# A written-out order for the first six steps of a recurrence and its router: a dozen moves, waits for a shared port, and router weights loaded earlier

## The chip, the cores and the metric

The kernel runs on one core of a Trainium2 chip. The core has five engines that work side by side, each on its own instructions in order: TensorE (PE in the profile, with its weight loads shown as PEld), VectorE (DVE), ScalarE (ACT), GpSimd (POOL) and SyncE (SP). SP issues nearly all the loads. The metric is the time of one execution on the device, in microseconds (us).

## The reference

Two stages follow each other, all in 32-bit floats. The first is a gated linear recurrence over 768 steps for 4 batches of 8 heads with 48 channels:

```
f = 1 / (1 + exp(-f_logit))
state = f[t] * state + outer(k[t], v[t])
y[t] = q[t] @ state
```

The second is a mixture of experts without dropping, over the 3072 rows that y makes with its heads side by side (384 columns). Each row goes to the one of 8 experts with the largest logit:

```
logits = x @ w_gate;  e = argmax(logits);  g = softmax(logits)[e]
out = g * (relu(x @ w1[e]) @ w2[e])
```

with w1[e] of 384 by 1024 and w2[e] of 1024 by 384.

## The kernel before

The recurrence is done in chunks of 128 steps. Twelve units of work are numbered 0 to 11: each is one chunk of two batches, which holds 16 heads, two to a slot of 128 partitions, in 8 slots of 128 steps. The units of one pair of batches are every second one, so the state of unit u comes from unit u - 2.

For one unit u the steps are these; the names are those that the change uses, with the line of the kernel before:

- lf, lk, lq, lv (L466, on SP): load f, k, q and v. The tiles are reused: f has two, k three, q four, v three. So a load waits for the last reader of an earlier unit's tile.
- exp and ln (L476, L484, on ACT): the negative logarithm of the gate.
- scan (L491, on DVE): its running sum over the chunk.
- r and dec (L505, L520, on ACT): the growth and the decay, exp of plus and minus the sum.
- byr (L509): k times r, on POOL (for unit 0 on DVE). byd (L532, on DVE): q times the decay.
- ends and last (L515, L527, on POOL): small copies of the last sum and the last decay.
- sc, in halves a and b (L543, on PE): scores of the chunk, k against q. mask (L549, on DVE): copies the causal ones to `at`.
- kp (L558, on PE) and keep (L563, on ACT): the transposed k, brought out of PSUM.
- wi, in halves (L571, on PE): the part of y from within the chunk. bef (L592, on PE): the part from the state before it.
- dp (L608, on PE): what the chunk adds to the state. upd (L623 or L625, on DVE) adds it to the old state, and updp (written upd..p; L627, on POOL) multiplies by the last decay.
- set (L633, on ACT): brings y out of PSUM. xp (L663, on PE): turns the rows and makes the logits in one product with a matrix that holds the router weights. The logits are summed over the slots on DVE (lg, L671), and lay (L688, L693, on ACT) brings the rows out.
- oh (choose, L214 to L222, on DVE), wgh (weigh, L254, on ACT), place (place and fill, L233 to L260, on DVE) and send (L189, indirect DMAs of POOL): the expert of each row, its place, and the scatter of the rows to DRAM, for two units at a time.

kp, dp, xp and a few others take turns at two banks of PSUM (`turns`), so each waits until what was two turns before is read.

The whole stage stands in an order written by hand (`manual_schedule`): on each engine the instructions run in the order in which the Python code issues them, and semaphores that the framework sets make an instruction wait for what it reads or overwrites. A first part of the code does units 0 and 1 and begins 2 and 3. Then a loop over n from 1 to 13 does the step n: the scores of unit n, the "within" and "before" of unit n - 1, the rows and logits of unit n - 2, and the elementwise work of units n + 1 to n + 3, with special cases for n = 1, 2 and 3.

The constants (`load_consts`, L174, 473.5 KB) and the router weights (`load_gate`, L180, four pieces of 6 KB) are written to one tile, `fpack`. The loop's products of k and r can be given one more wait: `by_r` (L507) takes an instruction out of the list `routed` and waits for it ("the port of both").

After the units, the eight experts follow, each with 24 groups of matmuls by w1 (`widen`, L316) and by w2 (`narrow`, L332); leftover rows are gathered in groups of 32 (L1081, L1107).

Of the kernel before, what the change touches and what calls it, by code (L numbers as in the profile page):

```python
# [1 line left out]

# [8 lines left out]
F32 = mybir.dt.float32  # L11
# [3 lines left out]
OP = mybir.AluOpType  # L15
# [103 lines left out]
def _bc(ap, axis, n):  # L119
    shape = list(ap.shape)  # L120
    shape.insert(axis, n)
    return ap[tuple([slice(None)] * axis + [None])].to_broadcast(shape)
# [3 lines left out]
def kernel(  # L126
# [41 lines left out]
    def load_first_consts():  # L168
        nc.scalar.dma_start(mpack, nc.inline_tensor(mv, name="c_mpack").ap())
        nc.scalar.dma_start(ident, fdram[:, slice(*fat["ident"])])  # L170
# [236 lines left out]
    def load_pads(e):  # L407
# [10 lines left out]
        tc.declare_no_dep(ins, group="xs", reason="no row is written twice")  # L418
        tc.add_to_no_dep_group("xs", ins)

    with ExitStack() as st:
        ld = st.enter_context(tc.tile_pool(name="ld", bufs=1))
        wk = st.enter_context(tc.tile_pool(name="wk", bufs=2))
# [21 lines left out]
            nc.vector.memset(g[:, :, 0:1], 0.0)  # L445
        units = [{} for _ in range(NU)]
        routed = []
        SYNC = mybir.DependencyInfo(mybir.DependencyClass.Sync, mybir.DependencyReason.DATA)
        states = [None, None]
        used = [0, 1]  # L450
# [6 lines left out]
        def load(u, names, parts=(slice(None),)):  # L457
            x = units[u]
            for n in names:
                src = {"q": qu, "k": ku, "f": fu, "v": vu}[n]  # L460
                if n == "v":
                    x[n] = ld.tile([128, 2, H, D], F32, name=n, bufs=3)
                else:
                    x[n] = held[n][u % len(held[n])]
                for part in parts:
                    nc.sync.dma_start(x[n][:, part], src[u][:, part])  # L466
# [19 lines left out]
        def total(u, part=whole):  # L486

            x = units[u]
            if "sum" not in x:
                x["sum"] = wk.tile([128, SEG, CR], F32, name="sum")  # L490
            nc.vector.tensor_tensor_scan(  # L491
                x["sum"][:, part].rearrange("p s c -> p (s c)"),
                x["g"][:, part].rearrange("p s c -> p (s c)"),
                cap[:, part].rearrange("p s c -> p (s c)"),
                0.0,
                OP.add,
                OP.min,
            )

        def growth(u, part=whole):  # L500

            x = units[u]
            if "r" not in x:
                x["r"] = wk.tile([128, SEG, C], F32, name="r", bufs=1)
            nc.scalar.activation(x["r"][:, part], x["sum"][:, part, 1:CR], AF.Exp)  # L505
# [8 lines left out]
        def ends(u):  # L514
            nc.gpsimd.tensor_copy(rend[:, u], units[u]["sum"][:, :, C])  # L515
# [7 lines left out]

        def last_decay(u):
            x = units[u]
            x["last"] = wk.tile([128, SEG], F32, name="last", bufs=3)
            nc.gpsimd.tensor_copy(x["last"], x["dec"][:, :, C - 1])  # L527

        def by_decay(u, part=whole):
            x = units[u]  # L530
            q = x["q"][:, part]
            nc.vector.tensor_tensor(q, q, x["dec"][:, part], op=OP.mult)  # L532

        def heads():
            return [(p, h, slice(DP * h, DP * h + DP)) for p in range(HP) for h in range(2)]
# [29 lines left out]
        def within(u, a):  # L565

            x = units[u]
            if a == 0:
                x["yt"] = yt
            for p, h, _ in heads():  # L570
                nc.tensor.matmul(  # L571
                    x["yt"][DP * (h ^ a) : DP * (h ^ a) + D, a, p],
                    lhsT=x["v"][:, a, 2 * p + h],
                    rhs=x["at"][:, a, h, p],
                    start=p == 0,
                    stop=x["old"] is None,
                    skip_group_check=True,
                )
# [38 lines left out]
        def update(u):  # L617

            x = units[u]
            new = wk.tile([128, SEG, D], F32, name="state", bufs=4)  # L620
            last = _bc(x["last"], 2, D)
            if x["old"] is None:
                nc.vector.tensor_copy(new, x["dp"])  # L623
            else:
                nc.vector.tensor_tensor(new, x["dp"], x["old"], op=OP.add)  # L625
            states[u % 2] = new
            return lambda: nc.gpsimd.tensor_tensor(new, new, last, op=OP.mult)  # L627

        def settle(u):
            x = units[u]  # L630
# [64 lines left out]
        st.enter_context(tc.manual_schedule(engines=ordered))  # L695

        nc.scalar.preload_act_table_set("natural_log_exp_and_others")
        load(0, "f", ab)
        load(0, "kq")
        load(1, "f")  # L700
        load_first_consts()
        load(1, "kq")
        for i in (1, 0):
            nc.gpsimd.memset(scores[i], 0.0)
        def warm(count):

            for _ in range(count):
                nc.tensor.matmul(yt[:, 0, 0], lhsT=pad[:, 0:C], rhs=pad[:, 0:C], start=True, stop=True)

        warm(24)  # L710
        for part in ab:
            steps(0, part)
            total(0, part)
        load(2, "f")
        load(0, "v")
        for part in ab:
            growth(0, part)
            by_r(0, part, nc.vector)
            decay(0, part)
            by_decay(0, part)  # L720
        ends(0)
        last_decay(0)
        for part in ab:
            steps(1, part)
        load(3, "f")
        load(2, "k")
        load(1, "v")
        load(2, "q")
        load(3, "q")

        def early_banks():

# [38 lines left out]
            del sends[: len(now)]  # L771


        score(0, 0)
        score(0, 1)
        keys(0)
        warm(12)
        for part in ab:
            total(1, part)
        for a in range(2):  # L780
            for h in range(2):
                mask(0, a, h)
        for part in ab:
            growth(1, part)
            by_r(1, part)
        for part in ab:
            decay(1, part)
            by_decay(1, part)
        ends(1)
        last_decay(1)  # L790
        steps(2)
        total(2)
        keep(0)
        steps(3, logs=False)
        growth(2)
        load_consts()
        load(3, "k")
        load(4, "f")
        load(2, "v")
        load(5, "f")  # L800
        load_gate()

        for n in range(1, NU + 2):
            here, back, last = n, n - 1, n - 2
            ahead = n + 1 < NU
            state = n < NU - 2
            rt = None
            if here < NU:
                units[here]["old"] = states[here % 2]
            if 2 <= last:  # L810
                settle(last)
            if later and later[0] < NU - 1:
                later[1].weigh()
            if here < NU:
                for a in range(2):
                    score(here, a)
            if ahead and n != 2:
                by_r(n + 1)
                ends(n + 1)
            if decayed:  # L820
# [3 lines left out]
                scatter_some(n)  # L824
            if n == NU - 2:
                soon = [load_rows(first[e]) for e in range(EARLY)]
            if n == 1:
                units[0]["old"] = None
                added(0)
                update(0)()  # L830
            if ahead and not 1 < n < 4:
                decay(n + 1)
                last_decay(n + 1)
            if state:
                keys(here)
                keep(here)
            if n == 2:
                growth(n + 1)
                by_r(n + 1)
                ends(n + 1)  # L840
            if 1 < n < 4:
                decay(n + 1)
                last_decay(n + 1)
            if here < NU:
                for a in range(2):
                    for h in range(2):
                        mask(here, a, h)
            if n == 1:
                log(3)
                within(0, 0)  # L850
                within(0, 1)
                settle(0)
            if n + 3 < NU:
                steps(n + 3)
            if later and n >= NU - 1:
                settled(*later)
                later = None
                scatter_some(NU)
            if 2 < n < NU - 2:
                total(n + 2)  # L860
            if n == NU - 2:
                by_decay(n + 1)
            first_half = 1 < n < NU - 2
            if first_half:
                within(back, 0)
            if 0 <= last:
                rt = rows(last, later[1] if later else None)
                lay(last)
            if later and n == NU - 2:
                settled(*later)  # L870
                later = None
                scatter_some(NU)
            if ahead and n < NU - 2:
                by_decay(n + 1)
            if n == 2:
                total(n + 2)
            if rt:
                rt.choose()
                if n < NU - 2:
# [7 lines left out]
            for a in range(int(first_half), 2):  # L887
                if 0 < back < NU:
                    within(back, a)
            if n == 2:  # L890
                settle(1)
            if n + 2 < NU and n != 1:
                growth(n + 2)
            if n == NU + 1:
                widen(soon[0], weights[0], early_h, range(3, 7))
# [2 lines left out]
            if state:  # L898
                added(here)
                decayed = update(here)  # L900
            if n == 1:
                total(3)
            if back < NU:
                before(back)
            if rt:
# [9 lines left out]
            if n == NU + 1:  # L915
                widen(soon[0], weights[0], early_h, range(7, NF))
                turn(soon[1])
            if n == 1:
                load(n + 3, "q")
            if n + 3 < NU:  # L920
                load(n + 3, "k")
            if n + 2 < NU:
                load(n + 2, "v")
            if 1 < n and n + 3 < NU:
                load(n + 3, "q")
            if n + 5 < NU:
                load(n + 5, "f")
            if n == 1:
                load_first_pads()
            if n in (8, 9):  # L930
                load_first_weights(n - 8)
                load_second_weights(n - 8)
# [395 lines left out]
```

## Time and profile before

| What | Value |
|---|---|
| median of 10 runs | 389.91 us (389.46 to 389.99) |
| the profiled execution's own time | 389.94 us |
| its span, first to last instruction | 388.2 us |
| busy: PE, DVE, ACT, POOL | 376.2, 169.3, 103.0, 115.8 us |
| DMA traffic | 95.05 MB, mean 245 GB/s |
| granted TensorE clock, mean | 0.997 |

A row of the timeline reads: start in us, time in us, engine, line, operation, what it writes and reads (out<-in), how many instructions were merged, and in brackets how long the engine had been idle before it and what ended that. SPq, ACTq and POOLq are instructions of an engine's queue, such as the issue of a DMA; the transfer itself lasts on after it. The chain is the work that ended last, followed back from the last instruction; it is printed in order of time. In the slices each digit is a fortieth of the span, 9.7 us, in tenths.

### The profile page before, as it was taken

The page shows a single profiled execution, that of the slowest core. Times are in us where ns is not written, and L with a number is a line of the kernel's source. Part 1 is how long each engine was busy: PE and PEld are TensorE (multiplying, and loading weights), DVE is VectorE, ACT ScalarE, POOL GpSimd, SP SyncE. Part 2 cuts the span into 40 slices and gives each one's busy share as a digit, 9 for nine tenths or more (in the row PEclk, how much of TensorE's full clock was granted, in tenths as well). Part 3 has the DMA queues.
Part 4 walks back from the last instruction along what each step waited for, and adds up shares of the span by engine and source line. Part 5 has one row for each costly group of instructions (what it writes and reads, how often), then busy time and mean ns, then how long its engine had stood idle before and what let it go on. Part 6 is the DMA issues. An engine that isn't in the chain of part 4 may idle for free.

```text
span 388.2 us, 7727 instructions
## 1 busy us (share of the span) xinstructions
PE 376.2 (97%) x3062; PEld 264.8 (68%) x3062; DVE 169.3 (44%) x365; ACT 103.0 (27%) x190; POOL 115.8 (30%) x118
## 2 busy tenths in 40 slices
PE   7988999999999999999999999999999999999993
PEld 7877899999989778685555555654466456555452
DVE  6998988889764632112121131115412113111360
ACT  6888878775432001010100110000010000001000
POOL 5378868887706710101102101100210210210113
PEclk9999999999999999999999999999999999999998
DMA  7999667868973659795559799899164359993141
GB/s 290 399 351 354 196 229 256 280 207 300 389 252 112 219 139 305 200 319 108 195 158 383 213 394 394 212 403 249 41 222 135 102 192 392 397 416 141 22 163 64
DMA packets 51516, 95.05 MB, mean 245 GB/s; under 512 B 20824, under 2 KB 40731, under 8 KB 49424
## 3 DMA queue, kind: packets, MB, share of 16 engines
q1 hardware_dynamic: 48016, 84.76, 64.5%
q0 software_dynamic: 3168, 9.64, 6.7%
q8 instruction: 25, 0.41, 0.4%
q14 instruction: 19, 0.16, 0.1%
q10 hardware_dynamic: 288, 0.08, 0.1%
HBM read 79.46 MB, written 15.21 MB: 244 GB/s over the span
## 4 chain that ended last, share of the span: by engine, by line
PE 88%; DMA 5%; DVE 2%; SPq 1%; issue 1%; ACT 1%; POOL 0%; POOLq 0%; DVEq 0%; ACTq 0%
PE hps L316 28%; PE yps L332 24%; PE yps L1107 7%; PE xp L663 6%; PE yt L571 5%; PE s L543 4%; PE s L316 3%; PE hps L1081 3%; PE yp L332 3%; PE yt L592 3%; DMA fpack<-c_fpack 2%; DMA f<-in_fu_dram 2%; PE dp L608 2%; PE kp L558 2%; DMA fpack<-in_moe_w_gate_dram 1%; SPq L466 1%
## 5 line engine op out<-in xcount | busy, mean ns | idle before, releaser
L316 PE MATMUL hps<-xT,w1t 128*128 128x352 f32 (+2 forms) x384 | 110.1, 447 | 0.0
L316 PEld LDWEIGHTS hps<-xT,w1t 128*128 128x128 f32 x384 | 72.7, 190 | 37.3 <-issue 2.2
L332 PE MATMUL yps<-w2t,hT 128*128 128x384 f32 x288 | 94.4, 487 | 0.0
L189 POOL DMA_INDIRECT out_dram<-ysb,dst x24 | 23.3, 972 | 222.3 <-DVE ysb L343 212.5
L332 PEld LDWEIGHTS yps<-w2t,hT 128*128 128x128 f32 x288 | 54.6, 190 | 38.6 <-issue 1.5
L326 ACT ACTIVATE hT<-hps 128x352 f32<-128x352 f32 (+2 forms) x28 | 13.7, 491 | 200.7 <-PE hps L316 190.6
L328 DVE TENSOR_SCALAR hT<-hps 128x352 f32<-128x352 f32 (+2 forms) x28 | 15.6, 558 | 92.9 <-PE hps L316 92.9
L343 DVE TENSOR_SCALAR ysb<-yps,tg 128x384 f32<-128x384 f32 x22 | 13.6, 618 | 74.4 <-PE yps L332 55.7
L189 POOL DMA_INDIRECT xs<-xr,posi x24 | 32.3, 1345 | 19.3 <-DVE counts L233 13.3
L549 DVE COPY_PREDICATED at<-mpack,s 128x512 f32<-128x512 uint8 x48 | 31.1, 728 | 6.1 <-PE s L543 6.1
L509 POOL TENSOR_TENSOR k<-k,r 128x1024 f32<-128x1024 f32 (+1 forms) x12 | 26.5, 2215 | 19.7 <-ACT r L505 10.3
L491 DVE TENSOR_TENSOR_SCAN sum<-g,cap 128x1032 f32<-128x1032 f32 (+1 forms) x14 | 28.8, 2058 | 2.9 <-ACT g L484 2.8
L1107 PE MATMUL yps<-qw,hqT 128*32 128x192 f32 (+1 forms) x192 | 26.8, 380 | 0.0
L663 PE MATMUL xp<-fpack,ys 128*128 128x104 f32 x192 | 25.1, 281 | 1.0 <-DMA fpack<-in_moe_w_gate_dram 0.8
L543 PE MATMUL s<-q,k 64*128 64x128 f32 x384 | 24.7, 278 | 1.4 <-POOL last L527 0.8
L571 PE MATMUL yt<-at,v 128*48 128x128 f32 x384 | 25.1, 276 | 0.0
L543 PEld LDWEIGHTS s<-q,k 64*128 64x128 f32 x384 | 22.4, 188 | 3.3 <-issue 1.5
L663 PEld LDWEIGHTS xp<-fpack,ys 128*128 128x128 f32 x192 | 22.7, 191 | 2.8 <-issue 1.3
L571 PEld LDWEIGHTS yt<-at,v 128*48 128x48 f32 x384 | 20.0, 123 | 2.6 <-issue 1.5
L1107 PE MATMUL yps<-w2t,hT 128*32 128x384 f32 x192 | 21.4, 487 | 0.0
L1107 PEld LDWEIGHTS yps<-w2t,hT 128*32 128x32 f32 x192 | 7.6, 110 | 13.0 <-issue 12.5
L532 DVE TENSOR_TENSOR q<-q,g 128x1024 f32<-128x1024 f32 (+1 forms) x14 | 16.4, 1174 | 0.0
(114 smaller groups left out, 361.6 us busy)
## 6 DMA issues: line engine op xcount, KB each, us to landing
qw<-in_moe_w_dram SPq DMA_DIRECT2D x16, 1536.0 KB, 12.3
w1t<-in_moe_w_dram SPq DMA_DIRECT2D x8, 1536.0 KB, 7.1
w2t<-in_moe_w_dram SPq DMA_DIRECT2D x8, 1536.0 KB, 12.6
k<-in_ku_dram SPq DMA_DIRECT2D x12, 512.0 KB, 4.7
q<-in_qu_dram SPq DMA_DIRECT2D x12, 512.0 KB, 5.7
f<-in_fu_dram SPq DMA_DIRECT2D x11, 512.0 KB, 6.0
xs<-pad SPq DMA_DIRECT2D x8, 600.0 KB, 4.4
v<-in_vu_dram SPq DMA_DIRECT2D x12, 384.0 KB, 4.9
```

The source lines that it names most:

```text
L189: ins = nc.gpsimd.indirect_dma_start(out=dst, out_offset=bass.IndirectOffsetOnAxis(ap=idx, axis=0), in_=src, in_offset=None, bounds_check= ...
L316: nc.tensor.matmul(x["h"][:, f], lhsT=w[0][:, j, b * 128 : b * 128 + 128], rhs=x["xT"][:, j], start=j == 0, stop=j == KD - 1,)
L328: nc.vector.tensor_scalar(to, x["h"], 0.0, None, op0=OP.max)
L332: nc.tensor.matmul(yp, lhsT=x["hT"][:, f, t * C : t * C + C], rhs=w[1][:, f, :], start=f == 0, stop=f == NF - 1,)
L491: nc.vector.tensor_tensor_scan(x["sum"][:, part].rearrange("p s c -> p (s c)"), x["g"][:, part].rearrange("p s c -> p (s c)"), cap[:, part ...
L509: ins = on.tensor_tensor(k, k, units[u]["r"][:, part], op=OP.mult).ins
L532: nc.vector.tensor_tensor(q, q, x["dec"][:, part], op=OP.mult)
L543: nc.tensor.matmul(ps[h][:, p], lhsT=x["k"][r, s], rhs=x["q"][r, s], start=True, stop=True)
L549: nc.vector.copy_predicated(x["at"][:, a, h], _bc(causal, 1, HP), x["ps", a][h])
L571: nc.tensor.matmul(x["yt"][DP * (h ^ a) : DP * (h ^ a) + D, a, p], lhsT=x["v"][:, a, 2 * p + h], rhs=x["at"][:, a, h, p], start=p == 0, st ...
L663: nc.tensor.matmul(xp[:, p], lhsT=x["ys"][:, a, p], rhs=wx[:, p, 0:XW] if a else wx[:, p, E:WX], start=True, stop=True,)
L1107: nc.tensor.matmul(yp[r], lhsT=h[:, f, at : at + T], rhs=w[:, f, cols], start=f == 0, stop=f == NF - 1, skip_group_check=True,)
```

## The change

The first part and the loop's steps n = 1 to 5 are replaced by a string of steps, `FIRST_STEPS`, that a small table of functions (`DO`) carries out one by one; the loop begins at n = 6. The same steps are there with the same shapes, but for six warm-up matmuls fewer (`fill6` for `warm(12)`), and a fourth buffer for `last`. By engine these are moved:

- PE: kp 2 stands between the two halves of score 2. In steps 3 and 5 both halves of "within" come before xp, and bef comes before dp.
- DVE: scan 5 comes before the masks of unit 3 instead of after them.
- ACT: ln 4 comes behind lay 0 (it was right behind exp 4), with ln 5 behind it.
- POOL: ends 0 comes behind k1's products; ends 3 before k3's; the state multiplications of units 2, 3 and 4 one or two places later; a send behind a small copy.
- SP: the four router weights' loads come right behind the constants, ahead of lk 3, lf 4, lv 2 and lf 5.

Besides, each k product of units 1 to 6 waits for the latest scan, q product, choice or placing issued before it on DVE (`port["latest"]`). In the loop before, only those behind a choice or a placing did (units 5 and on).

```diff
+    FIRST_STEPS = """
+        lf0a lk0 consts0 lq0 lf1 lk1 lq1 fill24 exp0a ln0a scan0a exp0b lf2 lv0 ln0b scan0b
+        r0a byr0a dec0a byd0a r0b byr0b dec0b byd0b last0 exp1a ln1a exp1b lf3 lk2 lv1 lq2
+        lq3 consts1 gate0 ln1b sc0a sc0b kp0 fill6 scan1a scan1b mask0a mask0b r1a byr1a r1b
+        byr1b ends0 dec1a byd1a dec1b byd1b ends1 last1 exp2 ln2 scan2 keep0 exp3 r2 sc1a
+        sc1b byr2 ends2 dp0 lk3 lf4 lv2 lf5 upd0 upd0p dec2 last2 kp1 lq4 lk4 keep1 mask1a
+        mask1b ln3 wi0a wi0b lv3 set0 exp4 lf6 pads0 byd2 dp1 upd1 scan3 sc2a upd1p kp2 sc2b
+        keep2 r3 ends3 byr3 dec3 last3 mask2a mask2b exp5 wi1a xp0 lay0 ln4 ln5 byd3 scan4
+        wi1b lk5 lv4 lq5 lf7 set1 r4 dp2 upd2 sc3a sc3b scan5 byr4 ends4 kp3 keep3 dec4
+        last4 mask3a mask3b exp6 ln6 wi2a wi2b lk6 lv5 xp1 lay1 byd4 oh1 r5 bef2 lq6 lf8 dp3
+        upd3 set2 wgh1 sc4a sc4b byr5 upd2p ends5 dec5 last5 kp4 keep4 mask4a mask4b scan6
+        exp7 ln7 wi3a xp2 lay2 byd5 place1 wi3b lk7 lv6 r6 dp4 upd4 bef3 lq7 lf9 set3 sc5a
+        sc5b byr6 upd3p ends6 upd4p dec6 last6 kp5 keep5 mask5a mask5b scan7 exp8 ln8 wi4a
+        wi4b lk8 lv7 xp3 lay3 byd6 oh3 r7 bef4 lq8 lf10 dp5 upd5 set4 wgh3 send5
+    """
...
+        port = {}
...
-            nc.vector.tensor_tensor_scan(
+            port["latest"] = nc.vector.tensor_tensor_scan(
...
-            x["last"] = wk.tile([128, SEG], F32, name="last", bufs=3)
+            x["last"] = wk.tile([128, SEG], F32, name="last", bufs=4)
...
-            nc.vector.tensor_tensor(q, q, x["dec"][:, part], op=OP.mult)
+            port["latest"] = nc.vector.tensor_tensor(q, q, x["dec"][:, part], op=OP.mult).ins
...
-        warm(12)
...
-        load_gate()
...
-        for n in range(1, NU + 2):
+        FIRST = 6
...
+        def do_choose(u, part):
+            routes[u].choose()
+            port["latest"] = routes[u].latest
+
+        def do_place(u):
+            settled(u + 3, routes[u])
+            port["latest"] = routes[u].latest
+
+        def do_by_r(u, part):
+            routed[:] = [port["latest"]] if u else []
+            by_r(u, piece(part), nc.gpsimd if u else nc.vector)
...
+        for what, u, part in re.findall(r"([a-z]+)(\d+)([abp]?)", FIRST_STEPS):
+            DO[what](int(u), part)
+        routed.append(routes[FIRST - 3].latest)
+        later, decayed = (FIRST - 1, routes[FIRST - 3]), waiting.pop(FIRST - 1)
+
+        for n in range(FIRST, NU + 2):
```

## The prediction

> **What bounds the kernel now.** I read the page's engine shares first, then the slices, then the chain that ended last, then the order of time over the first 46 us.
>
> ```profile
> PE 376.2 (97%) x3062; PEld 264.8 (68%) x3062; DVE 169.3 (44%) x365; ACT 103.0 (27%) x190; POOL 115.8 (30%) x118
> PE   7988999999999999999999999999999999999993
> DVE  6998988889764632112121131115412113111360
> PEclk9999999999999999999999999999999999999998
> DMA  7999667868973659795559799899164359993141
> ```
>
> TensorE is busy 97% of the span. Its idle time lies in the first slices, where VectorE (DVE) and the DMA engines are full. The chain says where TensorE takes over:
>
> ```profile
> 14.04 8.87 DMA fpack<-c_fpack
> ...
> 22.92 0.33 SPq L180
> ...
> 24.27 4.83 DMA fpack<-in_moe_w_gate_dram
> ...
> 29.19 2.02 PE xp L663 x16
> ...
> 41.88 1.14 PE dp L608 x32
> 43.02 1.02 PE yt L592 x32
> 44.04 1.99 PE s L543 x32
> ```
>
> From 41.88 to 382.3 every entry but about 0.1 us at 113.2 is TensorE, so each microsecond by which it is late or early at its first score of unit 4 (43.97 in the timeline) reaches the end whole. The change touches only what lies before and around that point. So the question is: when does score 4 start?
>
> Two facts of the opening decide it. The load queue is SP, strictly in order, and the DMA engines are full until about 41 us (share 1.02 and 409 GB/s in the stretch from 20 to 24 us):
>
> ```profile
> 14.04 1.08 SPq L174 DMA_DIRECT2D fpack<-c_fpack  x1
> 15.23 0.41 SPq L466 DMA_DIRECT2D k<-in_ku_dram  x1
> 16.02 0.40 SPq L466 DMA_DIRECT2D f<-in_fu_dram  x1
> 16.93 0.33 SPq L466 DMA_DIRECT2D v<-in_vu_dram  x1
> 19.12 0.33 SPq L466 DMA_DIRECT2D f<-in_fu_dram  x1
> 22.92 1.79 SPq L180 DMA_DIRECT2D fpack<-in_moe_w_gate_dram  x4
> 25.57 1.07 ACT L476 ACTIVATE g<-f 128x1024 f32<-128x1024 f32 x1 [1.10 <-DMA f<-in_fu_dram]
> ```
>
> and SP's own waits have
>
> ```profile
> SPq L180 <- DMA fpack<-c_fpack: 3.4, 1, 3.4
> ```
>
> The router weights (gate, L180) are written into the constants' tile, so SP stands 3.4 us until the constants have landed at 22.91. Before the change k3, f4, v2 and f5 were issued ahead of that stand (15.23 to 19.12). And f4 already arrives with no slack: ScalarE (ACT) waits 1.10 us for it and starts exp 4 at 25.57.
>
> **The change part by part.**
>
> *Router weights sooner.* The four gate pieces move ahead of k3, f4, v2 and f5; their wait for the constants' landing stays, as the built program shows. The constants are queued as before, behind the same transfers, so I keep their landing at 22.91. Then SP issues the gate from 22.92 (1.79 us) and k3 at 24.81, where q4 stands now. The DMA engines have meanwhile run dry. A 512 KB load into an idle queue took 3.4 us (q issued at 44.10), so k3 lands at 24.81 + 3.36 = 28.2. f4 follows by 512 KB at 409 GB/s, 1.28 us: 29.45. That is 3.9 us after the 25.5 of now. Bounds: the loads issued from 11.34 to 14.04 and the three in flight come to some 4.2 MB, 10.3 us at 409 GB/s, where 11.6 passed; had the constants landed that 1.3 us sooner, f4 lands at 28.1. With the 5.4 us of the f issued at 53.90 it lands at 25.27 + 5.4 = 30.7. I take 29.45, which uses the row of the like size into an empty queue. Gain of this part: the xp product's wait for the gate, 0.76 us, which sits on TensorE with slack (its next, dp 2, waits 1.02 us for ACT anyway): nothing. The others land in time: v2 30.4 for dp 2 at 35, f5 31.7 for exp 5 at 33.5, k4 about 34 for a product at 41.5.
>
> *The walk behind f4.* ACT's order becomes exp 4, keep 2, r 3, dec 3, exp 5, lay 0, ln 4, ln 5. With the pitches of the timeline (start to next start: exp 1.18, keep 0.95, r 0.96, dec 0.94, exp 1.18, lay 0.78) exp 4 starts at 29.45, keep 2 30.63, r 3 31.58, dec 3 32.54, exp 5 33.48, lay 0 34.66, ln 4 35.44 to 36.50. Beside it, POOL's k3 product runs 32.7 to 35.1 (2.37) and VectorE's q3 product, held by it, ends 1.09 later at 36.2, as it does now (32.17, 33.26). So scan 4 starts at 36.53 (33.18 now), takes 2.29, and ends 38.82. The state addition ends at 39.28.
>
> *Scan 5 ahead of mask 3, and k4's product behind scan 5.* Now scan 5 follows the masks and is held by POOL's product:
>
> ```profile
> 36.70 2.37 POOL L509 TENSOR_TENSOR k<-k,r 128x1024 f32<-128x1024 f32 x1 [1.04 <-ACT r L505]
> 38.31 2.92 DVE L491 TENSOR_TENSOR_SCAN sum<-g,cap 128x1032 f32<-128x1032 f32 x1
> 41.16 0.26 DVE L671 TENSOR_REDUCE lg<-xp 128x8 f32<-128x32 f32 x2
> 41.35 0.48 ACT L693 COPY xr<-xp 128x384 f32<-128x384 f32 x1 [0.23 <-DVE lg L671]
> ```
>
> A scan beside the product took 2.92, one alone 2.29: 0.63 saved. After: scan 5 39.19 to 41.48, mask 3 (2.59) to 44.0, lg 1 at 44.0, lay 1 at 44.19, dp 3 0.53 later at 44.72. The added wait makes k4's product run 41.5 to 43.9 on POOL; only small copies queue behind it, and score 4 needs it. q4's product ends at 45.5.
>
> *bef 2 ahead of dp 3; both halves of "within" ahead of xp 1.* No matmul is added. Now the wait for lay 1 stands idle (0.53 us) and bef's 1.02 us come after; moved, bef 2 lies in that wait. So score 4 starts right behind dp 3 (1.07): 44.72 + 1.07 = 45.79, against 43.97. TensorE's own row from score 3 at 36.35 says the same: score 1.99, kp 1.02 (its second half waits for the state addition, 39.3), within 2.02, xp 1.96, bef 1.02 end at 44.8. **Sum: +1.82 us.**
>
> *The moves with nothing on the path.* Kp 2 between the halves of score 2, ends 0 behind k1's product, the later state multiplications on POOL, four "last" buffers: all are covered by the wait for f4 (ACT idle from 24.5 to 29.45) or are needed several microseconds later. The waits of k1's product for scan 1 cost POOL about 0.5 us (12.72 becomes 13.25) and q1's product, and with it scan 2, 0.2; the same wait hides that. If f4 were in time, the 0.2 would count.
>
> *Six warm-up matmuls fewer.* They cost 1.4 us of an idle engine. TensorE then idles from about 14.3 to 16.6, and again about 2.7 us from 28.4 until keep 2 frees the bank of xp 0. Now the longest idle time between matmuls is 1.02 us. What idling costs shows in this trace: the first warm-up matmuls start every 0.213 us until 6.9 us and every 0.112 us after, and behind TensorE's last matmul (382.3) the granted clock reads:
>
> ```profile
> 382.30:385.80 3.50, 0.00 (x0) 0.00 (x0) 0.42 (x1) 0.00 (x0) 0.97 (x1) 1.00 0.11 32
> 385.80:388.20 2.40, 0.00 (x0) 0.00 (x0) 0.00 (x0) 0.00 (x0) 0.00 (x0) 0.51 0.02 7
> ```
>
> The third column from the end is the clock: full through 3.5 us of idling, then half. Idle times of 2.3 and 2.7 us lie between 1.02 and 3.5, so the bounds are 0 and one cold stretch. Cold from 31 to 36 us, xp 0 would end 1.7 us later and push lay 0 by about 0.3, score 3 some 2 us but still ahead of mask 3: +0.3 to +1.0. I take 0, since this row holds the clock for longer than either gap.
>
> [...]
>
> The profiled execution took 389.94 us with a span of 388.2; the median of the ten runs is 389.91. 389.94 + 1.82 = 391.76; against the median 391.7. The bounds of f4 carry over one to one: 28.1 gives +0.5, 30.7 gives +3.1.
>
> **The rivals.**
>
> *Faster: f4 is not late.* If the gate's wait on SP ended early enough that f4 still landed by 25.6, the rest of the change pays: exp 4 25.57, keep 2 26.75, r 3 27.70, dec 3 28.66, exp 5 29.6, lay 0 30.8, ln 4 until 32.65, scan 4 until 34.9, scan 5 35.3 to 37.6, mask 3 to 40.1, dp 3 40.85, score 4 41.9: −2.05, giving 387.9. Against it: the 3.4 us wait stands in the trace with its cause, and it would have to end 3.9 us sooner. It decides at f4 landing 29.45 − 1.82 = 27.6, the constants landing at 21.1.
>
> *No change:* the constants land about 1.8 us sooner; then delay and gain cancel, 389.9. For it: 1.3 us of their 8.9 are longer than the bytes ahead explain. Against it: nothing ahead of them in the queue has changed.
>
> *Slower still:* f4 lands as late as 30.7, or TensorE goes cold in the 2.7 us gap: 392.3 to 393.0.
>
> *The gate was the bound and the change does what it says:* the chain does pass through the gate's landing (24.27 to 29.10). But behind it VectorE's q3 product (31.34, 1.92 long) was held by POOL until 32.17 all the same, so 0.7 us of the gate's wait are not to be had.
>
> **How the numbers follow.** f4 late: 0.68 (391.7). Slower still: 0.12. No change: 0.06. Faster, f4 in time or nearly so: 0.14. A difference within 0.2% (0.8 us) is about what a measurement of this kernel can't tell from none; of the first case 0.04 fall in there, through an earlier landing. So faster 0.14, same 0.10, slower 0.76. The range leaves out most of the faster case and a little above the slowest: 389.2 to 393.3.
>
> **What would show it.** Right: SP idle until about 22.9 and then the gate ahead of k3 at about 24.8; a gap of some 3 us in the DMA traffic near 24 us; ACT waiting 4 to 5 us for f at exp 4 near 29.4; scan 4 near 36.5; score 4 near 45.8; from there TensorE without a gap. The scan of unit 5 should take 2.3, not 2.9. Wrong: exp 4 starting before 27.6, or TensorE waiting again behind 46 us (VectorE or POOL late by the new order), or matmuls at 0.21 us in the gaps' wake.

## The result, and the profile after

The changed kernel took 393.07 us (median of 8 runs, 392.67 to 393.50); the kernel before took 389.91 us (28 runs, 389.42 to 390.49). The ratio is 1.0082, with a 95% interval of 1.0073 to 1.0090: slower by 3.2 us. Twelve executions of the changed kernel are on record, the profiled one among them: 392.67 to 395.20 us. The profiled execution of the changed kernel took 392.67 us with a span of 390.7, against 389.94 and 388.2 before: +2.7 and +2.5.

Lines of the changed kernel lie lower by 18 or so: a load is L484, exp L494, ln L502, the scan L509, the k product L527, score L561, the constants L175, the router weights (gate) L181.

The page of the changed kernel, its span, engine shares and slices:

```profile
span 390.7 us, 7693 instructions
...
PE 377.1 (97%) x3050; PEld 265.4 (68%) x3050; DVE 169.6 (43%) x365; ACT 102.7 (26%) x190; POOL 110.5 (28%) x118
...
PE   7797999999999999999999999999999999999994
...
PEclk9899999999999999999999999999999999999999
DMA  7969868777983558977539899899154459994041
GB/s 284 380 208 368 305 194 283 229 247 278 391 300 105 205 152 253 267 256 169 191 90 400 206 400 394 222 398 285 40 189 165 102 170 390 397 415 157 12 173 62
```

TensorE's share says nothing of the loss: it is 97% in both kernels. (It counts 3050 matmuls instead of 3062: each of the six missing warm-up matmuls stands in the profile as two.) The slices do. The third DMA slice (19.5 to 29.3 us) falls to 208 GB/s between neighbours of 380 and 368, and PEclk has an 8 in the second slice, where before there was a 9. The first is the mechanism that was forecast; the second is one that the forecast had put at nothing.

The chain that ended last, in order of time (start, length, what), no longer passes through the gate's landing. It passes through f4:

```profile
17.22 3.58 PE s L561 x32
...
24.65 5.50 DMA f<-in_fu_dram
...
33.19 1.05 ACT g L538
34.24 1.04 ACT g L494 x2
...
36.09 1.91 ACT g L502 x2
...
39.36 0.54 DVE state L641
...
45.47 1.07 PE dp L625 x32
46.54 1.99 PE s L561 x32
```

SP's largest wait in the opening, from the waits of the changed kernel's queues (total, times, longest):

```profile
SPq L181 <- DMA fpack<-c_fpack: 6.8, 1, 6.8
```

And the timeline of the changed kernel behind it:

```profile
22.26 1.80 SPq L181 DMA_DIRECT2D fpack<-in_moe_w_gate_dram  x4
24.16 0.39 SPq L484 DMA_DIRECT2D k<-in_ku_dram  x1
24.65 0.38 SPq L484 DMA_DIRECT2D f<-in_fu_dram  x1
30.23 1.06 ACT L494 ACTIVATE g<-f 128x1024 f32<-128x1024 f32 x1 [3.98 <-DMA f<-in_fu_dram]
39.81 2.30 DVE L509 TENSOR_TENSOR_SCAN sum<-g,cap 128x1032 f32<-128x1032 f32 x1
42.02 2.59 DVE L567 COPY_PREDICATED at<-mpack,s 128x512 f32<-128x512 uint8 x4
44.48 0.29 DVE L689 TENSOR_REDUCE lg<-xp 128x8 f32<-128x32 f32 x2
```

SP stands for 6.8 us, where before it stood 3.4, because four loads that it used to issue first are now behind the stand. Meanwhile the DMA engines run dry; the windows of the two kernels over the same stretch (start:end, length, busy times, then clock, DMA share and GB/s) show it, the changed kernel first:

```profile
22.00:24.00 2.00, 1.92 (x24) 1.52 (x25) 2.00 (x4) 1.39 (x4) 2.00 (x3) 1.00 0.10 6
24.00:26.00 2.00, 2.00 (x54) 1.91 (x48) 2.00 (x3) 1.64 (x3) 0.64 (x2) 1.00 0.41 101
```

and the kernel before:

```profile
22.00:24.00 2.00, 1.77 (x48) 1.64 (x44) 2.00 (x3) 2.00 (x5) 2.00 (x2) 1.00 1.02 404
24.00:26.00 2.00, 1.67 (x29) 1.70 (x31) 2.00 (x3) 0.90 (x2) 2.00 (x3) 1.00 1.00 277
```

6 GB/s in place of 404. ScalarE then waits 3.98 us for f4 and starts exp 4 at 30.23 instead of 25.57. Score 4 starts at 46.47 instead of 43.97: +2.50. Behind it the two kernels run alike, but for 0.24 us more near 146 us and about as much won back behind the last matmul; the spans differ by 2.5.

### The profile page after: what moved, and what is told of

It reads as the page before. It is cut to its first block, busy times and chain, and to the rows that moved or that the text cites. A ratio compares the mean times of both kernels' runs of the same rounds, so it can differ in the third digit from the quotient of the medians.

```text
span 390.7 us, 7693 instructions
## 1 busy us (share of the span) xinstructions
PE 377.1 (97%) x3050; PEld 265.4 (68%) x3050; DVE 169.6 (43%) x365; ACT 102.7 (26%) x190; POOL 110.5 (28%) x118
## 4 chain that ended last, share of the span: by engine, by line
PE 90%; DMA 3%; ACT 3%; issue 1%; POOL 1%; DVE 1%; SPq 0%; POOLq 0%; ACTq 0%; DVEq 0%
PE hps L317 28%; PE yps L333 24%; PE yps L1119 7%; PE xp L681 6%; PE yt L588 5%; PE s L561 5%; DMA f<-in_fu_dram 3%; PE s L317 3%; PE hps L1093 3%; PE yp L333 3%; PE yt L609 3%; PE dp L625 2%; PE kp L576 2%; ACT g L502 1%; ACT g L494 1%
## 5 line engine op out<-in xcount | busy, mean ns | idle before, releaser
L317 PEld LDWEIGHTS hps<-xT,w1t 128*128 128x128 f32 x384 | 72.7, 190 | 37.5 <-issue 2.5
L527 POOL TENSOR_TENSOR k<-k,r 128x1024 f32<-128x1024 f32 (+1 forms) x12 | 26.2, 2184 | 24.9 <-ACT r L523 7.2
L509 DVE TENSOR_TENSOR_SCAN sum<-g,cap 128x1032 f32<-128x1032 f32 (+1 forms) x14 | 28.8, 2057 | 3.4 <-ACT g L502 2.8
L561 PE MATMUL s<-q,k 64*128 64x128 f32 x384 | 26.5, 290 | 3.1 <-POOL rend L533 2.7
L561 PEld LDWEIGHTS s<-q,k 64*128 64x128 f32 x384 | 24.0, 198 | 5.0 <-POOL rend L533 2.9
```

Of the source, the lines that this page charges most:

```text
L317: nc.tensor.matmul(x["h"][:, f], lhsT=w[0][:, j, b * 128 : b * 128 + 128], rhs=x["xT"][:, j], start=j == 0, stop=j == KD - 1,)
L509: port["latest"] = nc.vector.tensor_tensor_scan(x["sum"][:, part].rearrange("p s c -> p (s c)"), x["g"][:, part].rearrange("p s c -> p (s ...
L527: ins = on.tensor_tensor(k, k, units[u]["r"][:, part], op=OP.mult).ins
L561: nc.tensor.matmul(ps[h][:, p], lhsT=x["k"][r, s], rhs=x["q"][r, s], start=True, stop=True)
```

## The experiments

Three theories were put against each other. **L**: the late f4, behind SP's stand, is the loss; the rest of the change is a gain of some 2 us. **P**: the new order and its added waits (`port["latest"]`) cost time. **C**: the half clock that the six missing warm-up matmuls bring is the cause.

The runs were made in three groups, each on one chip and beside the kernel before on it. That took 401.07 us in the first group (e1 to e4), 401.56 in the second (e5 to e8) and 389.99 in the third (e9 to e12). What the first two chips add is told at the end; within a group the comparison holds.

### e1: the router weights back behind f5

```diff
-        lq3 consts1 gate0 ln1b sc0a sc0b kp0 fill6 scan1a ...
+        lq3 consts1 ln1b sc0a sc0b kp0 fill6 scan1a ...
-        sc1b byr2 ends2 dp0 lk3 lf4 lv2 lf5 upd0 ...
+        sc1b byr2 ends2 dp0 lk3 lf4 lv2 lf5 gate0 upd0 ...
```

> The changed kernel with the router weights' loads put back behind lf 5; all else as changed, six warm-up matmuls included. Theory L (the late f4 is the cause of the loss): f4 is in time, exp 4 starts by 26.5 us. But the changed kernel's trace shows score 1 at half the clock (3.58 us for 2.06), which the wait for f4 covered; uncovered it delays the state copy of unit 0 by about 2 us. So L with the cold clock gives the -2.05 us of the forecast's faster case plus some 1.6: 389.5 us against 389.9. L without it: 387.9. Rival P (the new order or the port's waits cost the time, the gate nothing): as changed, 393.

Measured: 401.54 us, ratio 1.0010 (0.9984 to 1.0035). The loss is gone, the gain is not there in the time. In the timeline it is: exp 4 starts at 25.19 and score 4 at 41.90. But the profiled execution, 399.07 us at a mean clock of 0.988, was the second shortest of twelve, and its score 1 ran at full clock; the four longest, 402.07 to 403.78 us, had mean clocks of 0.971 to 0.982.

### e2: the same, with twelve warm-up matmuls

The edit is that of e1 with `fill12` for `fill6`.

> As the run before, and with twelve warm-up matmuls again. L: 387.9 us, score 4 at about 41.9 us, score 1 in 2.06 us. P: 393 us. If the cold clock does not matter even here: the same as the run before.

Measured: 400.61 us, ratio 0.9995 (0.9977 to 1.0013), 0.9 us below e1; the intervals overlap. The mean clock of its twelve executions was 0.982 to 0.989 (0.978 to 0.989 in the kernel before on this chip), and score 4 of the profiled one started at 42.29.

### e3: only the warm-up restored

```diff
-        lq3 consts1 gate0 ln1b sc0a sc0b kp0 fill6 scan1a ...
+        lq3 consts1 gate0 ln1b sc0a sc0b kp0 fill12 scan1a ...
```

> The changed kernel with twelve warm-up matmuls again and the router weights early as changed. L: score 1 takes 2.06 us again, the state copy of unit 0 is 2 us sooner, but exp 4 still starts at about 30 us and the time stays within 0.4 us of the changed kernel's, 393.0. Rival C (the half clock is the cause of the loss): 391 us or less.

Measured: 405.54 us, ratio 1.0097 (1.0069 to 1.0125), +4.5 us. The timeline of e3:

```profile
31.80 1.06 ACT L494 ACTIVATE g<-f 128x1024 f32<-128x1024 f32 x1 [7.21 <-DMA f<-in_fu_dram]
```

The state of unit 0 is copied at 20.04 again, against 21.97 in the changed kernel, and ScalarE still waits for f4, 7.21 us here. With the warm-up back and the gate still early, the loss stays: C is not the cause of it. The profiled execution was the longest of the six, 408.80 us.

### e4: the kernel before, with only the router weights earlier

```diff
         load_consts()
+        load_gate()
         load(3, "k")
         load(4, "f")
         load(2, "v")
         load(5, "f")
-        load_gate()
```

> The kernel before with one thing changed: the router weights' loads right behind the constants. L: exp 4 starts at about 30 instead of 25.6 us, and ln 4, keep 2, r 3 and k3's product follow it there, so +3.6 to +4 us: 393.5 to 394. If the router weights were the bound and are worth having early: 389.2 (-0.7).

Measured: 406.26 us, ratio 1.0117 (1.0089 to 1.0145), +5.2 us. This one moved line carries the whole loss and more, without any of the new order. The timeline of e4:

```profile
22.66 2.89 SPq L180 DMA_DIRECT2D fpack<-in_moe_w_gate_dram  x4
...
30.76 1.06 ACT L476 ACTIVATE g<-f 128x1024 f32<-128x1024 f32 x1 [6.31 <-DMA f<-in_fu_dram]
...
33.52 3.74 PE L663 MATMUL xp<-fpack,ys 128*128 128x104 f32 x16 [5.12 <-ACT kn L563]
...
49.73 2.06 PE L543 MATMUL s<-q,k 64*128 64x128 f32 x32
```

ScalarE waits 6.31 us for f4, TensorE 5.12 us for ScalarE, and the first rows' product after that gap takes 3.74 us where 2.0 is usual. That is more than the 3.6 to 4 us that L expected: the profiled execution, the longest of the six at 407.64 us, has the half clock behind the gap, as that 3.74 us shows, and one piece of the gate took 1.53 us to issue where the others took 0.34 to 0.45. P is not needed for the loss, since the old order shows it; and the half clock here follows the late f4.

### e5: e2 again, beside the next three

> The kernel of the second run again, on another chip if there is one: on the first all kernels took some 11 us more, in waits of all engines around 120 to 132 us, and a gain of 2 us could not be told there, though score 4 started at 41.9 to 42.3 us. L: 2.05 us under the kernel before (score 4 at 41.9 to 42.3 against 43.97), a ratio of 0.995. Rival P: 1.00 or more.

Measured: 400.54 us, ratio 0.9970 (0.9944 to 0.9997); exp 4 at 24.91, scan 5 at 34.94 for 2.30, score 4 at 41.60.

### e6: e5 without the added waits

```diff
-            routed[:] = [port["latest"]] if u else []
+            routed[:] = [port["latest"]] if u > 4 else []
```

> As e5, with the added waits of k1's to k4's products taken out (those of units 5 and 6, which the kernel before has too, stay). If the order of scan 5 is what counts, scan 5 holds the port first in any case and k4's product starts behind it: within 0.3 us of e5. If the waits count: scan 5 takes 2.9 us again and the time is some 0.6 us over e5.

Measured: 400.64 us, ratio 0.9975 (0.9956 to 0.9994): e5's time to 0.1 us. The timeline of e6 shows why:

```profile
35.39 2.30 DVE L509 TENSOR_TENSOR_SCAN sum<-g,cap 128x1032 f32<-128x1032 f32 x1
36.25 3.60 POOL L527 TENSOR_TENSOR k<-k,r 128x1024 f32<-128x1024 f32 x1 [5.17 <-ACT r L523]
```

Without the wait k4's product starts 0.9 us into the scan and takes 3.60 us instead of the 2.37 it takes in e5. Counted from the start of the scan it ends after 4.46 us, and with the wait, in e5, after 4.90 (34.94 to 37.47 + 2.37). The scan, which came first, loses nothing either way: 2.30 us in both. So the wait adds 0.4 us on POOL, where nothing needs the product sooner, and protects a scan that was not in danger. On the whole time these runs can tell no difference, of either sign, of less than about 1 us: each interval reaches some 0.2 to 0.3% to either side.

### e7: e5 with scan 5 behind the masks again

```diff
-        ... sc3a sc3b scan5 byr4 ends4 kp3 keep3 dec4 last4 mask3a mask3b exp6 ...
+        ... sc3a sc3b byr4 ends4 kp3 keep3 dec4 last4 mask3a mask3b scan5 exp6 ...
```

> As e5, with scan 5 behind the masks of unit 3 again, as before (the latest operation that k4's product waits for is then scan 4, which it needs anyway). The forecast put 0.63 us on this part: 0.6 us over e5. Rival: mask 3 now ends sooner, lay 1 comes no later and the time is as e5.

Measured: 401.85 us, ratio 1.0001 (0.9984 to 1.0018): the gain of e5 gone, 1.3 us. The timeline of e7:

```profile
37.63 2.38 POOL L527 TENSOR_TENSOR k<-k,r 128x1024 f32<-128x1024 f32 x1 [5.55 <-PE kp L576]
39.27 2.91 DVE L509 TENSOR_TENSOR_SCAN sum<-g,cap 128x1032 f32<-128x1032 f32 x1
```

Here POOL came first, and the scan takes 2.91 us instead of 2.30. From scan 4 to score 4 it is 9.81 us in e7 (34.09 to 43.90) and 9.33 in e5 (32.27 to 41.60): 0.5 us of the order, against the 0.63 that was forecast. The rest of this execution's lag lies ahead of scan 4, beginning with a score 0 that started 0.9 us later, which the edit does not touch; so 0.5 us is what the trace shows of the order, and 1.3 us what the medians give. Ahead of dp 3, TensorE idles 0.40 us for lay 1 in e7 and not at all in e5: with scan 5 first, TensorE's own work is the limit there, and more than that wait can't be gained at this place.

### e8: the router weights early, but without their wait

The rows of the constants' tile that hold the router weights are loaded by themselves behind f2; the four pieces then need to wait only for that part (448 of the 947 columns).

```diff
-        nc.sync.dma_start(fpack[:, at:], fdram[:, at:])
+        nc.sync.dma_start(fpack[:, at:row], fdram[:, at:row])
+        nc.sync.dma_start(fpack[:, row + width :], fdram[:, row + width :])
...
-        ... ln0a scan0a exp0b lf2 lv0 ...
+        ... ln0a scan0a exp0b lf2 consts2 lv0 ...
-        lq3 consts1 gate0 ln1b sc0a sc0b kp0 fill6 scan1a ...
+        lq3 consts1 ln1b sc0a sc0b kp0 fill12 scan1a ...
-        sc1b byr2 ends2 dp0 lk3 lf4 lv2 lf5 upd0 ...
+        sc1b byr2 ends2 dp0 lk3 lf4 gate0 lv2 lf5 upd0 ...
```

> As e5, with the router weights' wait taken away rather than moved: the part of the constants that they are written into (448 of 947 columns) is loaded on its own behind lf 2, the rest at the old place, and the router weights come right behind lf 4, ahead of lv 2 and lf 5. L: f4 in time (exp 4 by 26.0 us), the router weights land by about 27 us instead of 29, xp 0 starts at 28.4 rather than 29.1, and the time is 0.3 to 0.6 us under e5. If early router weights are worth nothing: as e5. If loading them early costs whatever they wait for: over e5 by 2 us or more.

Measured: 400.44 us, ratio 0.9966 (0.9946 to 0.9986), 0.1 us from e5. Exp 4 starts at 25.57 and score 4 at 41.82. Router weights that come early without holding f4 up show no cost, and no gain over e5 either. The place that the change gave them, ahead of k3 and f4, was not tried without the wait.

### e9: the changed kernel, beside the next three

> The changed kernel itself, beside the next three on one chip. L (the late f4): f4 lands at 30 to 31, exp 4 starts behind it, score 4 starts at 46 to 47, and it is slower than before by 2.3 to 4.5 us (the first measurement gave 3.2, and the router weights alone in the earlier place gave 5.2). P (the order and the waits) and C (half clock) expect the same loss here, but ascribe it to other parts, so that the next three runs must keep it: P all three that contain the new order, C those with the six warm-up matmuls.

Measured: 394.27 us (393.72 to 395.29), ratio 1.0110 (1.0093 to 1.0128), +4.3 us. The profiled execution was the longest of the five, 395.29 us, and its timeline shows how the loss grows:

```profile
23.38 3.39 SPq L181 DMA_DIRECT2D fpack<-in_moe_w_gate_dram  x4
...
27.35 0.38 SPq L484 DMA_DIRECT2D f<-in_fu_dram  x1
...
32.38 1.06 ACT L494 ACTIVATE g<-f 128x1024 f32<-128x1024 f32 x1 [6.56 <-DMA f<-in_fu_dram]
...
34.05 3.66 PE L681 MATMUL xp<-fpack,ys 128*128 128x104 f32 x16 [3.91 <-ACT kn L581]
```

The constants landed at 23.36, the fourth piece of the gate alone took 2.03 us to issue (the others 0.34 to 0.45; why is open), and f4 landed at 32.30. Such a slow piece stands in e3 (1.31 us) and e4 (1.53 us) too, but not in the first profile of the change, nor in any run with the gate behind f4; e3, e4 and e9 are profiles of the longest execution of their run. TensorE idled 3.91 us ahead of the rows' product, which then ran at half clock (0.50 from 34.2 to 37.5). From exp 4 to scan 4 it is 7.18 us, against 6.90 in the first profile: 0.3 us for the second cold stretch, beside 2.15 for the later f4.

### e10: the changed kernel, with k3 and f4 alone ahead of the router weights

```diff
-        lq3 consts1 gate0 ln1b sc0a sc0b kp0 fill6 scan1a ...
+        lq3 consts1 ln1b sc0a sc0b kp0 fill6 scan1a ...
-        sc1b byr2 ends2 dp0 lk3 lf4 lv2 lf5 upd0 ...
+        sc1b byr2 ends2 dp0 lk3 lf4 gate0 lv2 lf5 upd0 ...
```

> The changed kernel with k3 and f4 alone issued ahead of the router weights; v2 and f5 stay behind them, and the warm-up stays at six. L: f4 is back at about 25, exp 4 at 24.9 to 25.6; f5 is issued near 24.6 and lands, as f4 did in the changed kernel, at about 30.1, where exp 5 wants it at 29.2 to 29.6, so exp 5, ln 4, scan 4 and score 4 come 0.5 to 1 us later than with all four ahead: score 4 at 42.2 to 43.0, and the time from 1.5 us below before to no difference. If instead the mere number of loads behind the stand counts, half of the loss stays: 1.5 us above before. P and C: as slow as the changed kernel.

Measured: 390.03 us (388.38 to 391.81), ratio 0.9997 (0.9980 to 1.0014). Two loads moved bring 4.2 of the 4.3 us. But the gain of the order is not there: score 4 of the profiled execution (391.16 us) starts at 44.39 instead of the 42.2 to 43.0 that L expected. Nor is the reason the one that L named, a late f5: f5 landed at 30.77 and exp 5 started at 31.66, behind ScalarE's own work. The timeline of e10:

```profile
16.95 3.79 PE L561 MATMUL s<-q,k 64*128 64x128 f32 x32 [3.07 <-POOL rend L533]
20.66 1.95 PE L625 MATMUL dp<-v,kn 128*64 128x48 f32 x32
23.47 1.08 ACT L581 COPY kn<-kp 128x512 f32<-128x512 f32 x2 [1.66 <-PE kp L576]
...
26.83 1.07 ACT L494 ACTIVATE g<-f 128x1024 f32<-128x1024 f32 x1
```

Exp 4 waits for no load any more. It is late because ScalarE waited 1.66 us for kp 1 from a TensorE at half clock: score 1 took 3.79 us instead of 2.06, dp 0 1.95 instead of 1.1. With f4 in time, the six missing warm-up matmuls have a price. The record of all twelve executions says so too: the five with a mean clock of 0.995 or more have a median of 389.38 us, the seven with 0.993 or less 391.01.

### e11: the new order and the added waits alone

The edit is e10's with `lv2 lf5` ahead of `gate0` too, and `fill12` for `fill6`; it is the kernel of e2 and e5.

> The changed kernel with the router weights behind f5 again and twelve warm-up matmuls, so the new order and the port waits alone: L: exp 4 at about 25, scan 5 at 2.3 us, score 4 at 41.6 to 42.3 against 43.97, and the time 1 to 2 us below before, the more of it the less TensorE stands later on. P: slower than before by 2 us or more.

Measured: 388.24 us (388.05 to 388.67), ratio 0.9956 (0.9944 to 0.9969): 1.75 us faster than before, and 6.0 us faster than the change as it was made. The timeline of e11:

```profile
16.79 2.06 PE L561 MATMUL s<-q,k 64*128 64x128 f32 x32 [1.84 <-POOL rend L533]
...
22.43 1.79 SPq L181 DMA_DIRECT2D fpack<-in_moe_w_gate_dram  x4
...
25.07 1.07 ACT L494 ACTIVATE g<-f 128x1024 f32<-128x1024 f32 x1 [0.64 <-POOL state L643]
...
28.76 2.00 PE L681 MATMUL xp<-fpack,ys 128*128 128x104 f32 x16 [0.17 <-DMA fpack<-in_moe_w_gate_dram]
...
35.28 2.30 DVE L509 TENSOR_TENSOR_SCAN sum<-g,cap 128x1032 f32<-128x1032 f32 x1
...
41.94 2.06 PE L561 MATMUL s<-q,k 64*128 64x128 f32 x32
```

The rows' product waits 0.17 us for the gate: that is all that an earlier gate could have brought here. P falls with this run.

### e12: the kernel before, with six warm-up matmuls fewer

```diff
-        warm(12)
+        warm(6)
```

> The kernel before with six warm-up matmuls in place of twelve, nothing else. TensorE then idles about 2.5 us ahead of score 1. C: half clock for 3.4 us behind it, score 1 at 3.6 us instead of 2.06, the state of unit 0 2 us later, and since here no late f4 covers this, up to 1.5 us of it at score 4, so 0.5 to 2 us slower than before. L: f4 stays at 25.5, and what the half clock delays is needed only by product dp 2 and the state addition; no difference, within 0.5 us.

Measured: 390.97 us (390.02 to 391.91), ratio 1.0023 (1.0012 to 1.0034), +1.0 us. C was right about this kernel and L wrong: where no late f4 covers it, the half clock costs. The timeline of e12, and its window behind the gap, with the clock in the third column from the end:

```profile
17.21 2.66 PE L543 MATMUL s<-q,k 64*128 64x128 f32 x32 [2.23 <-POOL last L527]
19.80 1.95 PE L608 MATMUL dp<-v,kn 128*64 128x48 f32 x32
...
18.50:21.50 3.00, 3.00 (x46) 2.78 (x43) 1.69 (x1) 2.50 (x5) 0.08 (x1) 0.50 1.02 400
```

The half clock began in the middle of score 1, so score 1 took 2.66 us and not the 3.6 that C expected, and dp 0 1.95. Score 4 started at 45.07, 1.10 later than in the kernel before; but 0.6 us of that was there at score 0 already, ahead of the gap, so the price stands on the times and not on this timeline. They split by the clock: of the twelve executions the five with a mean clock of 0.995 or more took 390.02 to 390.81 us, the seven with 0.994 or less 390.93 to 391.91. All 23 of the kernel before had 0.995 or more.

## Why the prediction was right, and where it was not

The forecast was 391.7 us, slower by 1.8, with 0.76 on slower. The direction, the cause and the path were right; the size was short by 1.4 us of the median (0.9 of the profiled execution's own time), inside the range, near the upper end of its 389.2 to 393.3. Of the 0.9, 0.7 lies ahead of score 4 (table below) and 0.2 in what the time counts outside the span.

| Step | forecast | first profile |
|---|---|---|
| constants landed | 22.91 | 22.24 |
| k3 issued | 24.81 | 24.16 |
| k3, issue to landing | 3.36 | 4.69 |
| f4 landed | 29.45 | 30.15 |
| exp 4 | 29.45 | 30.23 |
| keep 2 / r 3 / dec 3 | 30.63 / 31.58 / 32.54 | 31.29 / 32.23 / 33.19 |
| exp 5 / lay 0 / ln 4 | 33.48 / 34.66 / 35.44 | 34.14 / 35.18 / 35.95 |
| scan 4 / scan 5 | 36.53 / 39.19 | 37.13 / 39.81 |
| dp 3 | 44.72 | 45.40 |
| score 4 | 45.79 | 46.47 |

**The stand on SP.** Right, with its place and its consequence. e4 shows that it alone makes the loss, and e10 that of the four loads behind it k3 and f4 are those that matter.

**The landing of f4.** The term of the sum that was mis-sized. The constants came 0.67 us sooner than in the old profile, which by itself would have made f4 land at 28.8; but k3, into an empty queue, took 4.69 us instead of the 3.36 of the row it was taken from, and f4 followed 1.29 behind it (1.28 forecast). Together +0.70, within the upper bound of 30.7. It was luck that the constants came sooner: without it f4 would have landed at 30.8, past the bound. The row was of q at 44.10, with one load close behind it (f, from 44.52); here four were issued within 1.8 us. In the 2 us stretches from 24 the engines moved 101, 383 and 326 GB/s, so by k3's landing at 28.85 some 1.2 MB, more than twice its 512 KB: the loads behind k3 moved beside it. That this is the whole of its delay was not tested.

**The walk behind f4.** Right: 16.34 us from exp 4 to score 4 were forecast and 16.24 measured. Scan 5 took 2.30 us, as the row of a scan alone said. That the wait for f4 covers what the added waits and the other moves cost was right as well; e6 shows no cost of the waits even without that cover, within about 1 us. One reading was off without effect: behind 41.88 the chain of the old profile leaves TensorE for 0.7 us at 113.2, not 0.1 (TensorE itself idles 0.2 of it).

**The six warm-up matmuls.** Priced at 0 "since this row holds the clock for longer than either gap". That step failed. The gap ahead of score 1 was 2.73 us, and the windows of the changed kernel say what followed:

```profile
14.50:17.20 2.70, 0.00 (x0) 0.01 (x1) 2.70 (x5) 2.67 (x5) 2.70 (x4) 1.00 0.97 365
17.20:20.50 3.30, 3.28 (x32) 3.30 (x32) 2.72 (x2) 2.88 (x6) 0.59 (x2) 0.54 1.00 397
```

Score 1 took 3.58 us, and the state of unit 0 was copied at 21.97 instead of 19.70. By the trace it cost nothing at score 4 in this kernel, since ScalarE stood 3.98 us for f4 behind it; so the term of the sum held by its cover, which is luck, and not by the reason that was given. Its price without cover is e12's 1.0 us, and e10 shows it in the new order. So the rival that was priced for f4 in time had it wrong too. The second gap, forecast at 2.7 us, was 1.33 in the first profile, since the half clock had pushed TensorE's work ahead of it from 28.4 to 30.58; it was 3.91 in e9, where the cold stretch cost 0.3 us, the lower end of the +0.3 to +1.0 that was named.

The row was misread. In the changed kernel's profile the clock changed at 7.23, 17.47, 20.88 and 389.52: three, one and 108 times 3.41 us apart. In the old profile it changed at 6.95 and 385.83, 111 times 3.41 us apart. Counted in such steps, the last matmul ended at 382.27 and a step began at 382.42, so those 3.5 us were one whole idle step and the short rest of the step before, not a time for which the clock is always held: the first profile lost it behind 2.73 us. The gaps ahead of score 1, and what followed:

| Run | gap ahead of score 1 | score 1 took | clock shown |
|---|---|---|---|
| first profile of the changed kernel | 2.73 us | 3.58 us | 0.50 (17.47 to 20.88) |
| e9 | 2.48 us | 3.55 us | 0.50 (17.1 to 20.5) |
| e10 | 3.07 us | 3.79 us | 0.50 (17.1 to 20.5) |
| e12 | 2.23 us | 2.66 us | 0.50 (18.5 to 21.5) |
| e1 | 2.81 us | 2.06 us | 1.00 (16.7 to 19.0) |
| e11 | 1.84 us | 2.06 us | 1.00 (17.1 to 20.5) |
| e2, e5, e7, e8 (twelve warm-up matmuls) | 1.50 to 1.75 us | 2.06 us | – |

The length of the gap did not decide alone: e1 kept the full clock behind 2.81 us, and e12 lost it behind 2.23. In the first profile the whole gap (14.49 to 17.22) lay in one step, 14.06 to 17.47. That it counts how a gap lies over the steps is an estimate from that profile; the table does not show it. Nor did it take one long gap: late in e2 TensorE idled 3.06 us in six pieces between 121.46 and 127.82, the longest of 0.95, and the stretch from 125 to 140 has a clock of 0.66.

Executions of one kernel differ: the half clock began at 17.47 in the first profile and by 17.1 in e9, the same kernel. The times of e10 lie over 3.4 us and those of e11 over 0.6, and the two shortest of e10, 388.38 and 388.59, are times like e11's. The mean clock goes along: 0.997 in these two, 0.995 to 0.999 in all of e11, 0.990 to 0.992 in the four longest of e10. All executions of the changed kernel, the twelve and the five of e9, had 0.994 or less.

**The rivals.** "Faster: f4 is not late" was priced at −2.05 with score 4 at 41.9, giving 387.9. e11 is that case with the six warm-up matmuls put back: score 4 at 41.94 and 388.24 us, −1.75. With six fewer the times show no gain (1.0010 in e1, 0.9997 in e10). "No change" wanted the constants 1.8 us sooner; they came 0.67 sooner. "The gate was the bound" falls with e11's 0.17 us and with e8. "Slower still" named f4 at 30.7 or a cold TensorE in the second gap; e9's execution has both, with f4 at 32.30, past the bound.

**The median.** Of the +3.16 the first profile holds 2.73, since no execution on record is shorter than the profiled one. The traces show one way to a longer one, that of e3, e4 and e9: a piece of the gate that takes long to issue, a later f4 and a second cold stretch. How often it comes is open.

## What to carry to other kernels

SP issued in order in these runs, so a stand of 6.8 us ahead of four loads of 6 KB held up the four loads behind them, and exp 4 started at 30.23 us instead of 25.57. Before a small load is moved ahead of one that has no slack, look up what it waits for (here a write to a tile that another load still fills), and read how long its own consumer really waits for it, which was 0.2 to 0.8 us here. And warm-up matmuls that look idle may be holding the clock: ahead of score 1, gaps of up to 1.84 us kept the full clock here, and of the five gaps of 2.23 to 3.07 us four lost it. Read such gaps in the trace before matmuls are taken out, since the cover that hides a cold stretch can vanish with the next change.

## What the runs showed of the hardware

- The clock's changes, 3.41 us or a whole multiple of it apart in two profiles, and the half clock behind gaps, in the table above. In e10 the gap of 3.07 us was followed by a clock of 0.50 from 17.1 to 20.5 and of 0.91 from 20.5 to 34, which makes about 2.4 us more of half clock, though TensorE was busy throughout the first of these stretches.
- In the two pairs seen here, of a scan on VectorE and a k product on POOL that overlap, the one that came second took longer and the first did not: the product 3.60 us beside a scan of 2.30 (e6), the scan 2.91 beside a product of 2.38 (e7); with no overlap, in e5, they took 2.37 and 2.30. The kernel's name for the wait, "the port of both", gives a cause; the runs show these times.
- The chips of e1 to e4 and of e5 to e8 took some 11 us longer for the kernel before and for its variants. The traces put 9.9 of the 11.7 us between the spans of e5 and e11, the same kernel, into one stretch. The windows of e5 there:

```profile
115.00:125.00 10.00, 7.99 (x104) 7.13 (x104) 3.46 (x18) 2.19 (x6) 5.94 (x7) 1.00 0.32 110
125.00:140.00 15.00, 10.70 (x47) 8.83 (x47) 5.25 (x26) 1.62 (x5) 5.94 (x10) 0.77 0.21 80
```

and of e11, on the chip of e9 to e12:

```profile
115.00:125.00 10.00, 10.00 (x121) 9.63 (x116) 4.36 (x26) 2.81 (x8) 6.97 (x8) 1.00 0.33 125
125.00:140.00 15.00, 15.00 (x81) 11.15 (x80) 8.53 (x34) 0.60 (x1) 6.31 (x10) 1.00 0.56 183
```

  TensorE loses 6.3 us of 25 there, has a clock of 0.77 in the second stretch, and the DMA engines move 80 GB/s instead of 183. The waits of e5 name no engine for much of it. Its cause was not found. The rest comes ahead of it: at score 4 e5 is 0.3 us ahead of e11, at 102 us 1.4 behind. Of that 1.1 are lost near 60 us, where TensorE stops twice in the middle of a dp with no releaser (in e2, the same kernel, that dp lasts 2.21 us from 59.61, where e11's takes 1.07); e4, with the old order, loses 0.4 there against the first profile of the kernel before. So part of the smaller gain of the same kernel on that chip (−1.0 us in e5, −1.75 in e11) seems to be lost there; one trace of each can't settle it.
